# Layer two with tokens as the stationary operand, weights converted by their bits, exponentials slot by slot, and filler matmuls at the start

## The chip, the cores and the metric

The kernel runs on one core of a Trainium2 chip. The metric is the time of one execution in device microseconds, and the median of three runs is taken. A core has five engines that run their own instruction streams in order and wait for each other on semaphores: PE (TensorE, matmuls; its weight loads are shown as PEld), DVE (VectorE), ACT (ScalarE), POOL (GpSimd) and SP (SyncE, which here only issues DMAs).

## What is computed

Eight batches of 576 tokens pass through windowed attention with 8 heads of 64 and then through a gated two-layer network. Heads 0 to 3 look at the last 32 keys; heads 4 to 7 look at every fourth of the last 128 keys (dilated).

```python
scores = scale * np.matmul(q, k.transpose(0, 1, 3, 2))
scores = np.where(masks[None, :, :, :], scores, -1000000000.0)
scores = scores - np.max(scores, axis=-1, keepdims=True)
attn = np.exp(scores)
attn = attn / (np.sum(attn, axis=-1, keepdims=True) + 1e-09)
x = np.matmul(attn, v)                 # heads side by side: [8, 576, 512]
h = np.maximum(x @ w_in, 0.0)          # [8, 576, 1024]
conv_out = sum(conv_w[k] * hp[:, k:k + S, :] for k in range(3))   # hp: h padded by a zero row
gate = 1.0 / (1.0 + np.exp(-conv_out))
return h * gate @ w_out                # [8, 576, 512]
```

The three weight tensors come as 64-bit floats and are passed to the chip as pairs of 32-bit words.

## The kernel before

**Attention.** It works on pairs of heads, four pairs per batch: pairs 0 and 1 are plain (kind 0), pairs 2 and 3 dilated (kind 1). A pair is one piece of short matmuls for the scores (L248) into the PSUM tile `att`, a softmax on DVE and ACT in nine slots of 64 keys (L254 to L273), one piece of short matmuls for the values (L283), again into `att`, and copies that split the result into a high and a low part, `x..a` and `x..b` (L320, L333 to L337). `att` is one buffer, so scores and values take turns. For the first two batches (HELPED) the high part is subtracted on PE by matmuls with `minus`, a negated identity (L327, L330), and ACT copies the rest.

**The network.** Each product of two numbers is made of three terms (TERMS): high by high, high by low, low by high. Layer one (L353) has the weights stationary and 288 tokens moving: 8 blocks of the hidden width x 2 halves of the tokens x 4 slices x 3 terms = 192 matmuls per batch. ACT applies the relu into `h`, DVE and ACT make the convolution, the sigmoid and the gate, and `g..a` and `g..b` are its high and low parts. Layer two (L395) again has the weights stationary and 288 tokens moving: 4 x 2 x 8 x 3 = 192 matmuls per batch, with the output transposed. Over eight batches each layer has 1536 matmuls of 288 columns.

**The weights.** 16 blocks of 128x512 and the small `conv` are converted on ACT and DVE (`weights`, L413). For the first ten blocks (SUMMED) the low part is finished on PE: a 128x512 matmul in f32 (L450) and two in fp32r (L451, L452).

**The order.** Every piece of work is a task with a cost and a due time. `Planner.order` (L113) lists the tasks engine by engine from estimated costs, buffers and due times, and the program is written in that order. The due times are DUE, PAIR, WI and WO (L196 to L204). Outside the plan stand the first instructions: the DMA of the mask on ACT's queue, an identity, and five DVE copies that spread the mask (L465 to L479).

Of the kernel before, what the change touches and what calls it, by code (L numbers as in the profile page):

```python
# [34 lines left out]
F32 = mybir.dt.float32  # L35
# [10 lines left out]
NP = 4  # L46
# [27 lines left out]
class Planner:  # L74
# [38 lines left out]
    def order(self):  # L113
# [40 lines left out]
        return [t for _, t in sorted(done, key=lambda x: x[0])]  # L154
# [3 lines left out]
def attn_moe(ctx: ExitStack, tc: tile.TileContext, qk_p, qk_d, v_p, v_d, w_in, w_out, conv, mask, out):  # L158
# [37 lines left out]
    DUE = {0: (-9.2, 2.8, 30.4), 1: (64.7, 50.1, 92.3)}  # L196
    PAIR = {0: (-26.0, -24.7, -23.0, -27.0), 1: (-4.9, 1.3, 8.9, 14.5)}
    WI, WO = (-20.4, -20.4, -7.2, -7.2, -3.1, -0.1, 7.8, 7.8), (17.2, 17.2, 36.3, 36.3, 36.9, 34.9, 43.2, 43.2)
    AHEAD = (9.1, 0.8, 0.7)
    PERIOD = 55.1  # L200
    for b in range(2, B):
        DUE[b] = tuple(t + PERIOD * b for t in (-5.1, 5.4, 33.0))
        PAIR[b] = tuple(t + PERIOD * b for t in (-21.7, -18.8, -17.2, -13.1))
    SUMMED = 10  # L204
    HELPED = 2

# [21 lines left out]
    def attention(b, p):  # L228
        due = PAIR[b][p]
# [5 lines left out]
        lq = plan.add("SP", n * 0.0017, due - AHEAD[0], lambda: nc.sync.dma_start(  # L235
            out=qk.t[:, :n], in_=(qk_p, qk_d)[kind][b, p % 2]), uses=[qk])
        lv = plan.add("SP", 1.35, due - AHEAD[1], lambda: nc.sync.dma_start(
            out=v.t, in_=(v_p, v_d)[kind][b, p % 2]), uses=[v])

        def scores():  # L240
# [11 lines left out]
        flat = lambda: s.t.rearrange("p a k -> p (a k)")  # L252
        halves = lambda t: t.rearrange("p (h k) -> p h k", h=2)
        last = plan.add("DVE", 0.68, due + 1.5, lambda: nc.vector.tensor_tensor(  # L254
            out=halves(flat()[:, 0:512]), in0=sc.t[:, 0:2, 0:256], in1=halves(mask_sb[:, kind, 0:512]), op=ALU.add),
            [last], [sc, s])
        last = plan.add("DVE", 0.215, due + 1.5, lambda: nc.vector.tensor_tensor(  # L257
            out=flat()[:, 512:576], in0=sc.t[:, 2, 0:W], in1=mask_sb[:, kind, 512:576], op=ALU.add), [last], [sc, s])
        wide = lambda t: t.unsqueeze(2).to_broadcast([128, 9, W])
        last = plan.add("DVE", 0.755, due + 2.0, lambda: nc.vector.tensor_reduce(  # L260
            out=m.t, in_=s.t, axis=AX.X, op=ALU.max), [last], [s, m])
        last = plan.add("DVE", 0.755, due + 2.5, lambda: nc.vector.tensor_tensor(
            out=s.t, in0=s.t, in1=wide(m.t), op=ALU.subtract), [last], [s, m])
        last = plan.add("ACT", 0.685, due + 3.0, lambda: nc.scalar.activation(
            out=s.t, in_=s.t, func=AF.Exp, scale=SCALE), [last], [s], "exp")
        last = plan.add("DVE", 0.755, due + 3.5, lambda: nc.vector.tensor_reduce(
            out=z.t, in_=s.t, axis=AX.X, op=ALU.add), [last], [s, z])
        last = plan.add("DVE", 0.173, due + 3.6, lambda: nc.vector.tensor_scalar(
            out=z.t, in0=z.t, scalar1=1e-9, scalar2=None, op0=ALU.add), [last], [z])
        last = plan.add("DVE", 0.215, due + 3.7, lambda: nc.vector.reciprocal(out=z.t, in_=z.t), [last], [z])  # L270
        last = plan.add("DVE", 0.755, due + 3.8, lambda: nc.vector.tensor_tensor(  # L271
            out=s.t, in0=s.t, in1=wide(z.t), op=ALU.mult), [last], [s, z])
        last = plan.add("DVE", 0.755, due + 4.5, lambda: nc.vector.transpose(out=pt.t, in_=flat()), [last], [s, pt])  # L273
# [29 lines left out]
        last = plan.add("PE", (0.9, 0.85)[kind], due + 6.0, values, [lv, last], [v, pt, tv, x], "V")  # L303

        def parts(t):

            if kind == 0:
                return (t[:, 0:512].rearrange("c (q m) -> c q m", q=4), t[:, 512:S].rearrange("c (g m) -> c g m", g=2))
            t = t.rearrange("c (m r) -> c r m", r=RES)
            return t[:, :, 0:128], t[:, :, 128:RL].rearrange("c (g r) m -> c g r m", g=2)  # L310

        def src(i):
            if i == 0:
                return tv.t[:, :, 0:128]
            rest = tv.t[:, 0:2, 128:160]
            return rest if kind == 0 else rest.rearrange("c g (r m) -> c g r m", r=2)

        his = []
        for i, cost in ((1, (0.25, 0.3)[kind]), (0, (0.62, 1.12)[kind])):
            last = plan.add("ACT", cost, due + 7.0, lambda i=i: nc.scalar.copy(out=parts(x.t[0])[i], in_=src(i)),  # L320
                            [last, *his], [tv, x])
            his.append(last)
        if b < HELPED:
            def less():
                main, rest = parts(x.t[0])
                for t in range(4):
                    nc.tensor.matmul(tv.t[:, t, 0:128], minus, main[:, t], start=False, stop=True,  # L327
                                     skip_group_check=True)
# [3 lines left out]
            last = plan.add("PE", (0.42, 0.6)[kind], due + 7.2, less, his, [tv, x], "E")
            return [plan.add("ACT", cost, due + 7.5, lambda i=i: nc.scalar.copy(out=parts(x.t[1])[i], in_=src(i)),  # L333
                             [last], [tv, x]) for i, cost in ((0, (0.62, 1.12)[kind]), (1, (0.25, 0.3)[kind]))]
        return [plan.add("DVE", cost, due + 7.5, lambda i=i: nc.vector.tensor_tensor(
            out=parts(x.t[1])[i], in0=src(i), in1=parts(x.t[0].bitcast(F32))[i], op=ALU.subtract), his, [tv, x])
            for i, cost in ((0, (0.68, 1.0)[kind]), (1, (0.215, 0.25)[kind]))]  # L337
# [3 lines left out]

    def expert(b, ready, wired, wored, conved):
        due, gated, out_due = DUE[b]
        x = [xs[b, p] for p in range(NP)]
        h, c, g = ([Buffer(n) for _ in range(NF)] for n in "hcg")
        relu = []
        for u in range(2 * NF):
# [3 lines left out]
            def first(fc, hf, ps, k):  # L351
                for i, (jw, jx) in enumerate(TERMS):
                    nc.tensor.matmul(ps.t[:, 0:HALF], wi[jw][fc][:, k * 128:k * 128 + 128],  # L353
                                     x[k].t[jx][:, hf * HALF:hf * HALF + HALF],
                                     start=(k == 0 and i == 0), stop=(k == NC - 1 and i == 2))

            for k in range(NC):
                last = plan.add("PE", 0.396, due + 1.6 * u + 0.4 * k, lambda a=(fc, hf, ps, k): first(*a),
                                [last, wired[fc], *(ready[k] if b == 0 else sum(ready, []))], [ps, x[k]], "E")
# [9 lines left out]
        for fc in range(NF):  # L369
# [4 lines left out]
            for k in (0, 2):  # L374
# [5 lines left out]
            hi = plan.add("ACT", 0.675, d + 2.0, lambda fc=fc: nc.scalar.copy(out=g[fc].t[0], in_=c[fc].t),  # L380
                          [t], [c[fc], g[fc]])
            lo = plan.add("DVE", 0.755, d + 2.5, lambda fc=fc: nc.vector.tensor_tensor(
                out=g[fc].t[1], in0=c[fc].t, in1=g[fc].t[0].bitcast(F32), op=ALU.subtract), [hi], [c[fc], g[fc]])
            gates.append(lo)

        for dm in range(NC):
            o = Buffer("out")
            outs = []
            for hf in range(2):
                u = 2 * dm + hf  # L390
                ps, last = Buffer("nn"), None

                def second(dm, hf, ps, k):
                    for i, (jw, jg) in enumerate(TERMS):
                        nc.tensor.matmul(ps.t[:, 0:HALF], wo[jw][2 * dm + k // 4][:, k % 4 * 128:k % 4 * 128 + 128],  # L395
                                         g[k].t[jg][:, hf * HALF:hf * HALF + HALF],
                                         start=(k == 0 and i == 0), stop=(k == NF - 1 and i == 2))

                for k in range(NF):
                    last = plan.add("PE", 0.396, out_due + 3.3 * u + 0.4 * k, lambda a=(dm, hf, ps, k): second(*a),  # L400
                                    [last, wored[2 * dm + k // 4], gates[k]], [ps, g[k]], "E")
# [11 lines left out]
    def weights(src, n, due, dst=None, pair=None, summed=False):  # L413
# [10 lines left out]
        def step(cost, uses, run):  # L424
            return plan.add("DVE", 0.16 + cost * f, due, run, [last], uses)
# [141 lines left out]
```

## Time and profile before

| what | value |
|---|---|
| time, median of 3 runs (lowest, highest) | 549.82 us (549.78, 550.69) |
| span of the profiled execution, first to last instruction | 549.1 us |
| its busy time: PE, DVE, ACT | 522.4, 415.7, 298.1 us |
| DMA | 52.31 MB, mean 95 GB/s |

The time of the profiled execution itself is not listed apart from its span; the span is 0.7 us below the median of the runs. Times in rows of the timeline count from the start of the span. A matmul's record runs from its start to its modelled end, and consecutive ones overlap, so its price in a stream is the distance from start to start. One f32 matmul is two records, so "x72" is 36 matmuls; some records are missing.

### The profile page before, as it was taken

To read this page: it belongs to the slowest core of one execution; us is meant where nothing else is said; L and a number is where in the kernel's file an instruction comes from. 1 tells how busy PE (TensorE), PEld (TensorE's weight loads), DVE (VectorE), ACT (ScalarE), POOL (GpSimd) and SP (SyncE) were. 2 spreads that over 40 slices of the span, in tenths; PEclk is the share of its full clock that TensorE was granted. 3 is DMA by queue.
4 is the path that set the end of the run, shared out by engine and by line. 5 is a ranking of instruction groups with operands and counts; after the bars stand their busy time and mean duration, and the time that the engine had idled before them with its cause. 6 is when DMAs were issued, how large, how long until landed. Compare 5 with 4: busy or idle time off the path is not lost.

```text
span 549.1 us, 19084 instructions
## 1 busy us (share of the span) xinstructions
PE 522.4 (95%) x8664; PEld 497.2 (91%) x8664; DVE 415.7 (76%) x695; ACT 298.1 (54%) x556; POOL 0.9 (0%) x12
## 2 busy tenths in 40 slices
PE   3499978999999999999999999999999999999997
PEld 2468876999999999999999999999989999999997
DVE  4968998899997389946998389946988389946920
ACT  2457784855752486337742486237742486337721
POOL 0000000000000000000000000000000000000000
PEclk9999996999999999999999999999999999999999
DMA  7756513331044102630055102530045102300011
GB/s 247 268 157 215 195 52 137 119 121 44 7 138 152 30 23 65 200 110 23 13 161 170 32 23 72 190 113 23 17 152 162 45 23 58 117 26 23 0 44 44
DMA packets 17072, 52.31 MB, mean 95 GB/s; under 512 B 2016, under 2 KB 3168, under 8 KB 16992
## 3 DMA queue, kind: packets, MB, share of 16 engines
q1 hardware_dynamic: 16848, 51.02, 27.8%
q8 instruction: 68, 1.11, 0.9%
q10 hardware_dynamic: 144, 0.08, 0.1%
q14 instruction: 12, 0.10, 0.1%
HBM read 41.66 MB, written 9.44 MB: 93 GB/s over the span
## 4 chain that ended last, share of the span: by engine, by line
PE 92%; DVE 3%; ACT 2%; DMA 2%; issue 1%; ACTq 0%
PE nn L395 38%; PE mm L353 35%; PE att L283 8%; PE att L248 6%; PE nn L450 2%; PE nn L353 2%; PE att L327 1%; DMA qk<-in_qk_d_dram 1%; DMA qk<-in_qk_p_dram 1%; PE nn L451 0%; PE nn L452 0%; DVE pt L273 0%; DVE s L271 0%; PE att L330 0%; DVE c L365 0%
## 5 line engine op out<-in xcount | busy, mean ns | idle before, releaser
L365 DVE SCALAR_TENSOR_TENSOR c<-h,conv_sb,c 128x576 f32<-128x576 f32 x128 | 103.9, 815 | 48.4 <-ACT c L371 46.9
L360 ACT ACTIVATE h<-mm 128x288 f32<-128x288 f32 x120 | 48.8, 408 | 50.4 <-PE mm L353 50.1
L402 ACT COPY out<-nn 128x288 f32<-128x288 f32 x64 | 25.5, 400 | 70.1 <-PE nn L395 66.1
L378 DVE TENSOR_TENSOR c<-c,h 128x576 f32<-128x576 f32 x64 | 47.6, 755 | 9.4 <-ACT c L376 7.8
L283 PEld LDWEIGHTS att<-pt,v 32*64 32x64 f32 x3072 | 40.8, 138 | 14.8 <-DVE s L257 4.6
L283 PE MATMUL att<-pt,v 32*64 32x64 f32 (+2 forms) x3072 | 44.2, 232 | 9.4 <-DVE s L257 3.5
L371 ACT ACTIVATE c<-h,conv_sb 128x576 f32<-128x576 f32 x64 | 49.7, 776 | 1.3
L248 PE MATMUL att<-qk 64*32 64x64 f32 x2432 | 36.2, 235 | 11.0 <-DMA qk<-in_qk_d_dram 5.5
L248 PEld LDWEIGHTS att<-qk 64*32 64x32 f32 x2432 | 30.2, 111 | 16.9 <-DMA qk<-in_qk_d_dram 5.5
L376 ACT ACTIVATE c<-c 128x576 f32<-128x576 f32 x64 | 42.5, 678 | 2.1 <-DVE c L365 1.6
L353 PE MATMUL mm<-x2a,wi 128*128 128x288 f32 x144 | 40.5, 296 | 0.0
L353 PE MATMUL mm<-x1a,wi 128*128 128x288 f32 x144 | 40.3, 296 | 0.0
L353 PE MATMUL mm<-x3a,wi 128*128 128x288 f32 x144 | 40.3, 295 | 0.0
L353 PE MATMUL mm<-x0a,wi 128*128 128x288 f32 x144 | 40.3, 295 | 0.0
L395 PE MATMUL nn<-g2a,wo 128*128 128x288 f32 x128 | 37.0, 304 | 0.0
L395 PE MATMUL nn<-g0a,wo 128*128 128x288 f32 x128 | 36.4, 299 | 0.2
L395 PE MATMUL nn<-g6a,wo 128*128 128x288 f32 x128 | 36.6, 299 | 0.0
L395 PE MATMUL nn<-g3a,wo 128*128 128x288 f32 x128 | 36.4, 299 | 0.0
L395 PE MATMUL nn<-g1a,wo 128*128 128x288 f32 x128 | 36.4, 299 | 0.0
L395 PE MATMUL nn<-g4a,wo 128*128 128x288 f32 x128 | 36.4, 299 | 0.0
L395 PE MATMUL nn<-g5a,wo 128*128 128x288 f32 x128 | 36.4, 299 | 0.0
L395 PE MATMUL nn<-g7a,wo 128*128 128x288 f32 x128 | 36.1, 300 | 0.1
(194 smaller groups left out, 1502.5 us busy)
## 6 DMA issues: line engine op xcount, KB each, us to landing
qk<-in_qk_d_dram SPq DMA_DIRECT2D x16, 664.0 KB, 4.4
qk<-in_qk_p_dram SPq DMA_DIRECT2D x16, 592.0 KB, 4.9
out_dram<-out SPq DMA_DIRECT2D x28, 288.0 KB, 2.2
v<-in_v_d_dram SPq DMA_DIRECT2D x16, 384.0 KB, 3.4
v<-in_v_p_dram SPq DMA_DIRECT2D x16, 384.0 KB, 3.5
out<-in_w_in_dram SPq DMA_DIRECT2D x8, 512.0 KB, 4.5
out<-in_w_out_dram SPq DMA_DIRECT2D x8, 512.0 KB, 4.2
out_dram<-out SPq DMA_DIRECT2D x8, 144.0 KB, 1.8
```

The costliest lines, as they stand in the source:

```text
L248: nc.tensor.matmul(sc.t[quad * 32:quad * 32 + 32, slot // 4, slot % 4 * W:slot % 4 * W + W], q, k, start=i == 0, stop=i == len(parts) - 1, ...
L283: nc.tensor.matmul(tv.t[hd * 64:hd * 64 + 64, bank, o:o + n], v.t[quad * 32:quad * 32 + 32, block // 2, block % 2 * 64:block % 2 * 64 + 64 ...
L327: nc.tensor.matmul(tv.t[:, t, 0:128], minus, main[:, t], start=False, stop=True, skip_group_check=True)
L353: nc.tensor.matmul(ps.t[:, 0:HALF], wi[jw][fc][:, k * 128:k * 128 + 128], x[k].t[jx][:, hf * HALF:hf * HALF + HALF], start=(k == 0 and i = ...
L360: relu.append(plan.add("ACT", 0.4, due + 1.6 * u + 1.6, lambda fc=fc, hf=hf, ps=ps: nc.scalar.activation(out=h[fc].t[:, 1 + hf * HALF:1 + ...
L365: nc.vector.scalar_tensor_tensor(out=c[fc].t, in0=h[fc].t[:, k:S + k], scalar=conv_sb[:, k, fc:fc + 1], in1=c[fc].t, op0=ALU.mult, op1=ALU ...
L371: t = plan.add("ACT", 0.777, d, lambda fc=fc: nc.scalar.activation(out=c[fc].t, in_=h[fc].t[:, 1:S + 1], func=AF.Copy, scale=conv_sb[:, 1, ...
L376: t = plan.add("ACT", 0.686, d + 1.0, lambda fc=fc: nc.scalar.activation(out=c[fc].t, in_=c[fc].t, func=AF.Sigmoid), [t], [c[fc]], "sigmoid")
L378: t = plan.add("DVE", 0.755, d + 1.5, lambda fc=fc: nc.vector.tensor_tensor(out=c[fc].t, in0=c[fc].t, in1=h[fc].t[:, 1:S + 1], op=ALU.mult ...
L395: nc.tensor.matmul(ps.t[:, 0:HALF], wo[jw][2 * dm + k // 4][:, k % 4 * 128:k % 4 * 128 + 128], g[k].t[jg][:, hf * HALF:hf * HALF + HALF], ...
L402: outs.append(plan.add("ACT", 0.4, out_due + 3.3 + 3.3 * u, lambda hf=hf, ps=ps, o=o: nc.scalar.copy(out=o.t[:, hf * HALF:hf * HALF + HALF ...
L450: nc.tensor.matmul(ps.t, ident, t(), start=True, stop=False)
```

## The change

1. **Layer two** (L431 to L464 of the new kernel): 128 tokens of `g` are stationary and 512 columns of `w_out` move. The first batch does it in two halves of 256 columns. Two consecutive batches share the tiles `g`: the even one leaves its first 64 tokens there, and the odd one joins them with its own first 64 into one block of 128 tokens. Together there are 768 matmuls of 512 columns and 192 of 256. The output is written as tokens by width.
2. **Weights** (`weights`, L491): 8 blocks of 128x1024, and the three PE matmuls are gone. High and low parts are cut out by shifts, masks and one multiplication. `conv` has its own steps (`few_weights`).
3. **Softmax** of the first eight pairs, two batches (SLOTS): the maximum goes into the exponential as a per-partition bias, slot by slot, in nine ACTIVATE of 64 columns that also sum. The subtraction and the sum on DVE are gone for these pairs. For the other 24 pairs 1e-9 stands in a 65th column, and the sum takes it in.
4. **Copies** of the dilated pairs into `x` and out of it are walked in another order of axes.
5. **Fillers** (`filled`, `fill`): where the plan has PE idle in its first 90 us, bf16 matmuls of 256 columns with an identity `eye` go into an unread part of `att`. There are 192 of them, 173 ahead of the first matmul of layer one.
6. **Due times**: a table DUE with one number for each task.

```diff
+    def filled(self, done, fill, since, until, unit, slack):
+        at, more = since, []
+        for s, t in done:
+            if t.engine == "PE" and s < until:
+                n = int((s - at - slack) / unit)
+                if n > 0:
+                    more.append((at, Task("PE", n * unit, at, lambda n=n: fill(n), (), (), None)))
+                at = s + t.cost
...
+        if slotwise:
+            last = plan.add("ACT", 0.23, soft + 1.0, lambda: nc.scalar.mul(out=m.t, in_=m.t, mul=SCALE), [last], [m])
+
+            def exps():
+                for i in range(9):
+                    nc.scalar.activation(out=s.t[:, i, 0:W], in_=s.t[:, i, 0:W], func=AF.Exp, bias=m.t[:, i:i + 1],
+                                         scale=SCALE, accum_out=z.t[:, i:i + 1])
...
-                        nc.tensor.matmul(ps.t[:, 0:HALF], wo[jw][2 * dm + k // 4][:, k % 4 * 128:k % 4 * 128 + 128],
-                                         g[k].t[jg][:, hf * HALF:hf * HALF + HALF],
...
+                    nc.tensor.matmul(ps.t[:, 0:n], g[k // 2].t[:, k % 2, jg, c0:c0 + 128],
+                                     w.rearrange("p h c -> p (h c)") if hf is None else w[:, hf],
...
-            def add():
-                nc.tensor.matmul(ps.t, ident, t(), start=True, stop=False)
-                nc.tensor.matmul(ps.t, minus, r.t, start=False, stop=False)
-                nc.tensor.matmul(ps.t, minus, hi, start=False, stop=True)
...
+        left = step(0.69, [load], lambda: nc.vector.tensor_scalar(
+            out=bits(lw), in0=bits(lw), scalar1=9, scalar2=None, op0=ALU.logical_shift_right))
+        left = step(1.22, [left], lambda: nc.vector.scalar_tensor_tensor(
+            out=bits(lw), in0=bits(hw), scalar=23, in1=bits(lw), op0=ALU.logical_shift_left, op1=ALU.bitwise_or))
+        last = step(0.69, [top, left], lambda: nc.vector.tensor_scalar(
+            out=bits(hw), in0=bits(t), scalar1=-0x800000, scalar2=None, op0=ALU.bitwise_and))
...
+    nc.vector.tensor_copy(out=eye, in_=ident)
...
+            nc.tensor.matmul(att[:, 3, 256:512], eye, eye.unsqueeze(1).to_broadcast([128, 2, 128]), start=not begun,
+                             stop=True, skip_group_check=True)
...
-        for t in plan.order():
+        for t in plan.filled(plan.order(), fill, 2.0, 90.0, 0.109, 0.35):
```

The first place is PE's start. Before, its stream begins with the four scores pieces of the first batch and the first values piece (`qk` queries and keys, `pt` transposed weights of the softmax, `v` values):

```order
L248 MATMUL att_159<-qk_98 32x64 x40
L248 MATMUL att_159<-qk_99 32x64 x36
L248 MATMUL att_159<-qk_98 32x64 x36
L248 MATMUL att_159<-qk_99 32x64 x40
L283 MATMUL att_159<-pt_112,v_100 64x64 x24
```

Now pairs of a weight load and a filler stand ahead of each piece; the lines left out are such pairs alone, 15 fillers ahead of the first scores, 13 and 34 ahead of the next two:

```order
L558 LDWEIGHTS eye
L558 MATMUL att_125<-eye 128x256
...
L270 MATMUL att_125<-qk_80 32x64 x36
L558 LDWEIGHTS eye
L558 MATMUL att_125<-eye 128x256
...
L270 MATMUL att_125<-qk_81 32x64 x40
L558 LDWEIGHTS eye
L558 MATMUL att_125<-eye 128x256
...
L270 MATMUL att_125<-qk_80 32x64 x40
```

So the first scores stand behind 15 matmuls that read `eye`.

The second place is DVE's start. Before, the five mask copies are followed at once by the first softmax:

```order
L476 COPY mask_sb<-kinds_sb 128x64
L254 TENSOR_TENSOR s_103<-att_159,mask_sb 128x512
L257 TENSOR_TENSOR s_103<-att_159,mask_sb 128x64
L260 TENSOR_REDUCE m_106<-s_103 128x9
L262 TENSOR_TENSOR s_103<-s_103,m_106 128x576
```

Now the six steps of `conv` (tiles `few`) and the copy that makes `eye` stand between:

```order
L540 COPY mask_sb<-c_117 128x64
L479 TENSOR_SCALAR few_78<-few_78 128x24
L480 TENSOR_SCALAR few_79<-few_78 128x24
L482 SCALAR_TENSOR_TENSOR few_79<-few_raw,few_79 128x24
L484 TENSOR_SCALAR few_78<-few_79 128x24
L486 SCALAR_TENSOR_TENSOR few_78<-few_raw,few_78 128x24
L488 TENSOR_TENSOR conv_sb<-few_79,few_78 128x24
L531 CAST eye<-pt_94 128x128
L282 TENSOR_TENSOR s_85<-att_125,mask_sb 128x8x64
L282 TENSOR_TENSOR s_85<-att_125,mask_sb 128x64
```

So `eye` comes after the mask copies and after `conv`, on the engine that everything at the start needs.

The third place is layer two on PE in the second half of the program. Before, three matmuls per slice of the hidden width, 288 columns each:

```order
L395 MATMUL nn_163<-g5a,wo_89 128x288
L395 MATMUL nn_163<-g5b,wo_89 128x288
L395 MATMUL nn_163<-g5a,wo_97 128x288
L395 MATMUL nn_163<-g6a,wo_89 128x288
L395 MATMUL nn_163<-g6b,wo_89 128x288
```

Now, with 512 columns (a row with x2 is the high and the low part of `g`, which are one tile):

```order
L443 MATMUL nn_129<-wo_74,g_112 128x512 x2
L443 MATMUL nn_129<-wo_76,g_112 128x512
L443 MATMUL nn_129<-wo_74,g_113 128x512 x2
L443 MATMUL nn_129<-wo_76,g_113 128x512
L443 MATMUL nn_128<-wo_73,g_110 128x512 x2
```

Where before four blocks of the output width had two halves of the tokens each, there are now four or five blocks of tokens, each as wide as the output.

More of the change, by code (lines that the diff above doesn't have):

```diff
@@ L273, in attention @@
-        last = plan.add("DVE", 0.755, due + 4.5, lambda: nc.vector.transpose(out=pt.t, in_=flat()), [last], [s, pt])
+        flat = lambda: s.t[:, :, 0:W]
+        halves = lambda t: t.rearrange("p (h a) k -> p h a k", h=2)
+        scored = lambda: (sc.t[:, 0:2, 0:256].rearrange("p h (a k) -> p h a k", k=W), sc.t[:, 2, 0:W])
+        two = lambda t: (halves(t[:, 0:8]), t[:, 8])
+        masked = mask_sb[:, kind].rearrange("p (a k) -> p a k", k=W)
+        wide = lambda t: t.unsqueeze(2).to_broadcast([128, 9, W])
@@ L275, in values @@
+        last = plan.add("DVE", 0.215, soft + 2.2, lambda: nc.vector.reciprocal(out=z.t, in_=z.t), [last], [z])
+        last = plan.add("DVE", 0.755, soft + 2.3, lambda: nc.vector.tensor_tensor(
+            out=flat(), in0=flat(), in1=wide(z.t), op=ALU.mult), [last], [s, z])
+        last = plan.add("DVE", 0.775, soft + 3.0, lambda: nc.vector.transpose(
+            out=pt.t.rearrange("p (a k) -> p a k", k=W), in_=flat()), [last], [s, pt])
         def values():
@@ L332, in attention @@
[L332 to L335, printed above, removed]
+                    nc.tensor.matmul(tv.t[:, g, 128:160], minus,
+                                     rest[:, g] if kind == 0 else rest[:, :, g].rearrange("c m r -> c r m"), start=False,
+                                     stop=True, skip_group_check=True)
@@ L336, in attention @@
+            last = plan.add("PE", 0.6, val + 1.2, less, his, [tv, x], "E")
+            return [plan.add("ACT", cost, val + 1.5, lambda i=i: nc.scalar.copy(out=parts(x.t[1])[i], in_=src(i)),
+                             [last], [tv, x]) for i, cost in pieces]
+        return [plan.add("DVE", cost + 0.06 * (1 - i), val + 1.5, lambda i=i: nc.vector.tensor_tensor(
             out=parts(x.t[1])[i], in0=src(i), in1=parts(x.t[0].bitcast(F32))[i], op=ALU.subtract), his, [tv, x])
-            for i, cost in ((0, (0.68, 1.0)[kind]), (1, (0.215, 0.25)[kind]))]
+            for i, cost in pieces]
@@ L384, in expert @@
             gates.append(lo)
[L386 to L395, printed above, removed]
-                                         g[k].t[jg][:, hf * HALF:hf * HALF + HALF],
[L397 to L401, printed above, removed]
-                outs.append(plan.add("ACT", 0.4, out_due + 3.3 + 3.3 * u, lambda hf=hf, ps=ps, o=o: nc.scalar.copy(
-                    out=o.t[:, hf * HALF:hf * HALF + HALF], in_=ps.t[:, 0:HALF]), [last], [ps, o]))
-                if b == B - 1:
-                    plan.add("SP", 0.6, out_due + 4.0 + 3.3 * u, lambda dm=dm, hf=hf, o=o: nc.sync.dma_start(
-                        out=out[b, dm, :, hf * HALF:hf * HALF + HALF], in_=o.t[:, hf * HALF:hf * HALF + HALF]),
-                        [outs[-1]], [o])
-            if b < B - 1:
-                plan.add("SP", 1.2, out_due + 4.0 + 6.6 * dm, lambda dm=dm, o=o: nc.sync.dma_start(
-                    out=out[b, dm], in_=o.t[:, :S]), outs, [o])
@@ new lines, in few_weights, with step @@
+    def few_weights(src, due):
+        u, t = few
+        low, high = (few_raw[:, :, i] for i in range(2))
+        ui, ti = u.bitcast(I32), t.bitcast(I32)
+        def step(run, after, engine="DVE"):
+            return plan.add(engine, 0.2, due, run, [after])
+        last = plan.add("SP", 0.1, due - 2.0, lambda: nc.sync.dma_start(
+            out=few_raw, in_=src.bitcast(I32).rearrange("p (n t) -> p n t", t=2)))
+        last = step(lambda: nc.scalar.activation(out=u, in_=high.bitcast(F32), func=AF.Abs), last, "ACT")
+        last = step(lambda: nc.vector.tensor_scalar(out=u, in0=u, scalar1=2.0 ** -15, scalar2=None, op0=ALU.max), last)
+        last = step(lambda: nc.vector.tensor_scalar(
+            out=ti, in0=ui, scalar1=3, scalar2=0x3fffffff, op0=ALU.logical_shift_left, op1=ALU.bitwise_and), last)
+        last = step(lambda: nc.vector.scalar_tensor_tensor(
+            out=ti, in0=high, scalar=-0x40000000, in1=ti, op0=ALU.bitwise_and, op1=ALU.bitwise_or), last)
+        last = step(lambda: nc.vector.tensor_scalar(
+            out=ui, in0=ti, scalar1=-0x800000, scalar2=None, op0=ALU.bitwise_and), last)
+        last = step(lambda: nc.vector.scalar_tensor_tensor(
+            out=u, in0=low.bitcast(U32), scalar=2.0 ** -52, in1=u, op0=ALU.mult, op1=ALU.mult), last)
+        return step(lambda: nc.vector.tensor_tensor(
+            out=conv_sb.rearrange("p t c -> p (t c)"), in0=t, in1=u, op=ALU.add), last)
@@ new lines, in weights, with step @@
+    def weights(src, due, fetch, hi, lo):
+        raw, tb = Buffer("raw"), Buffer("t")
+        part = lambda i: raw.t.rearrange("p (n w) -> p n w", w=2)[:, :, i]
+        lw, hw = (lambda i=i: part(i).bitcast(F32) for i in range(2))
+        t = lambda: tb.t
+        shaped = lambda x, like: x.rearrange("p (a c) -> p a c", a=like.shape[1])
+        whole = lambda x: x.rearrange("p a b c -> p a (b c)") if len(x.shape) == 4 else x
+        hi, lo = whole(hi), whole(lo)
+        bits = lambda x: x().bitcast(I32)
+        load = plan.add("SP", 3.0, fetch, lambda: nc.sync.dma_start(
+            out=raw.t, in_=src.bitcast(I32)), uses=[raw])
+        def step(cost, after, run):
+            return plan.add("DVE", cost, due, run, after, [raw, tb])
+        last = plan.add("ACT", 1.14, due, lambda: nc.scalar.activation(out=t(), in_=hw(), func=AF.Abs), [load], [raw, tb])
+        last = step(0.69, [last], lambda: nc.vector.tensor_scalar(
+            out=t(), in0=t(), scalar1=2.0 ** -15, scalar2=None, op0=ALU.max))
+        last = step(0.69, [last], lambda: nc.vector.tensor_scalar(
+            out=bits(t), in0=bits(t), scalar1=3, scalar2=0x3ffff000,
+            op0=ALU.logical_shift_left, op1=ALU.bitwise_and))
+        top = step(1.22, [last], lambda: nc.vector.scalar_tensor_tensor(
+            out=bits(t), in0=bits(hw), scalar=-0x40000000, in1=bits(t), op0=ALU.bitwise_and, op1=ALU.bitwise_or))
+        high = plan.add("ACT", 1.14, due, lambda: nc.scalar.copy(out=hi, in_=shaped(t(), hi)), [top], [tb])
+        left = step(0.69, [load], lambda: nc.vector.tensor_scalar(
[4 more added lines that the diff above has]
+            out=bits(hw), in0=bits(t), scalar1=-0x800000, scalar2=None, op0=ALU.bitwise_and))
+        return [high, plan.add("DVE", 1.22, due, lambda: nc.vector.scalar_tensor_tensor(
+            out=lo, in0=shaped(lw().bitcast(U32), lo), scalar=2.0 ** -43, in1=shaped(hw(), lo),
+            op0=ALU.mult, op1=ALU.mult), [last], [raw])]
@@ L465, in attn_moe @@
+    ident = pts[0][0][:, 0:128]
+    kinds_sb = cs[0][0].bitcast(BF16)[:, 0:5 * W].rearrange("p (a k) -> p a k", k=W)
     nc.scalar.dma_start(out=kinds_sb, in_=mask)
```

243 lines of the change are left out of this document (127 added, 116 removed).

## Prediction

> **What bounds the kernel now.** I read the page from the top: span, busy times, slices, the chain of work that ended last.
>
> ```profile
> span 549.1 us, 19084 instructions
> PE 522.4 (95%) x8664; PEld 497.2 (91%) x8664; DVE 415.7 (76%) x695; ACT 298.1 (54%) x556; POOL 0.9 (0%) x12
> PE   3499978999999999999999999999999999999997
> PE 92%; DVE 3%; ACT 2%; DMA 2%; issue 1%; ACTq 0%
> ```
>
> PE carries 92% of the chain and is short of 9 tenths only in the first slices and the last. A busy PE is not yet PE doing needed work, so the windows come next (length; busy time and instructions by engine; granted clock, DMA).
>
> ```profile
> 0.00:98.66 98.66, 76.82 (x1672) 64.91 (x1673) 82.72 (x161) 57.95 (x109) 0.90 (x12) 0.95 0.52 180
> 98.66:140.00 41.34, 41.34 (x377) 41.08 (x377) 38.03 (x65) 25.86 (x48) 0.00 (x0) 1.00 0.25 85
> 305.80:367.45 61.65, 61.65 (x1074) 59.68 (x1074) 47.25 (x76) 33.33 (x62) 0.00 (x0) 1.00 0.27 89
> ```
>
> From 98.66 us PE never rests; a steady batch takes 61.65 us, with DVE at 47.25 and ACT at 33.33. So there are two stages: a start that DVE, ACT and DMAs shape, and a body that only PE's own work shortens. I therefore count that work at its steady price and call the rest lost. From the chain in order of time (start, length, what, matmuls):
>
> ```profile
> 38.80 1.29 PE att L283 x81
> 114.61 19.09 PE nn L395 x144
> 333.63 0.90 PE att L248 x58
> 342.39 1.06 PE att L248 x66
> 347.22 1.19 PE att L283 x77
> ```
>
> One matmul of 288 columns costs 19.09 / 144 = 0.1326 us; both layers have 2 x 1536, so 407.3 us. Scores cost 0.90 (plain) or 1.06 (dilated), values 1.29 or 1.19; two of each in eight batches make 16 x 4.44 = 71.0 us. Returning from such a piece costs more, as PE's timeline shows:
>
> ```profile
> 333.33 0.29 PE L395 MATMUL nn<-g1a,wo 128*128 128x288 f32 x1
> 333.56 0.97 PE L248 MATMUL att<-qk 64*32 64x64 f32 x72
> 334.46 0.40 PE L395 MATMUL nn<-g2a,wo 128*128 128x288 f32 x1
> 334.70 0.29 PE L395 MATMUL nn<-g2b,wo 128*128 128x288 f32 x1
> ```
>
> 333.33 to 334.70 is 1.37 us; less 0.90 and two starts of 0.13 that leaves 0.2 us. Both orders have 55 returns: 11.0 us. The weight sums and the subtractions by `minus`:
>
> ```profile
> 28.04 2.08 PE L450 MATMUL nn<-w0b,ident 128*128 128x512 f32 x2
> 30.76 1.89 PE L450 MATMUL nn<-w1b,ident 128*128 128x512 f32 x2
> 48.82 1.02 PE L450 MATMUL nn<-w0b,ident 128*128 128x512 f32 x2
> 49.91 0.39 PE L452 MATMUL nn<-wi,minus 128*128 128x512 f32 x1
> 50.14 0.29 PE L353 MATMUL mm<-x1a,wi 128*128 128x288 f32 x1
> 97.90 0.63 PE L327 MATMUL att<-x1a,minus 128*128 128x128 f32 x4
> 98.51 0.38 PE L395 MATMUL nn<-g0a,wo 128*128 128x288 f32 x1
> ```
>
> One weight sum takes 48.82 to 50.14, 1.32 us, ten of them 13.2. A subtraction takes 97.90 to 98.51, 0.61 us, eight of them 4.9. **PE's work before** is 407.3 + 71.0 + 11.0 + 13.2 + 4.9 = 507.4 us. The last matmul ends at 545.6 (tail, below), so **38.2 us are lost**, nearly all before 98.66 us. Part of that is a slow clock: the same three matmuls of a sum took 28.04 to 30.76, 2.72 us, 2.06 times the later price.
>
> **The change, part by part.** The **weight sums** go: -13.2 us of PE.
>
> **Layer two** becomes 768 matmuls of 512 columns and 192 of 256. The trace has a 512-column fp32r matmul: 49.91 to 50.14, 0.23 us. Against 0.1326 at 288 that is 0.000435 us per column, so 256 columns cost 0.1187. 768 x 0.23 + 192 x 0.1187 = 199.4, against 1536 x 0.1326 = 203.7: -4.3 us. Starts are printed to 0.01, so 0.225 to 0.235 bounds it: -8.1 to -0.5. I take the row.
>
> PE's work after is 507.4 - 13.2 - 4.3 = 489.9 us. In the body I expect no new waits: a layer-two block now lasts 24 x 0.23 = 5.5 us instead of 3.2, so two open blocks cover the last gate's chain better, and ACT's wider copies have its slack to hide in.
>
> **The start** is the uncertain part. First, `eye`. Rows of DVE, PE and ACT, then groups (count, busy, mean ns):
>
> ```profile
> 5.47 1.61 PE L248 MATMUL att<-qk 64*32 64x64 f32 x80 [5.47 <-DMA qk<-in_qk_d_dram]
> 5.64 0.45 DVE L472 COPY mask_sb<-kinds_sb 128x576 bf16<-128x576 bf16 x1 [5.64 <-DMA kinds_sb<-in_mask_dram]
> 6.60 0.17 DVE L476 COPY mask_sb<-kinds_sb 128x64 bf16<-128x64 bf16 x1
> 39.32 0.23 ACT L428 ACTIVATE w0a<-out 128x24 f32<-128x24 f32 x1
> 39.58 0.18 DVE L430 TENSOR_SCALAR w0a<-w0a 128x24 f32<-128x24 f32 x1 [1.00 <-ACT w0a L428]
> 40.73 0.18 DVE L457 TENSOR_TENSOR conv_sb<-w0b,w0a 128x24 f32<-128x24 f32 x1
> ```
>
> ```profile
> L371 ACT ACTIVATE c<-h,conv_sb 128x576 f32<-128x576 f32 x64 | 49.7, 776 | 1.3
> L376 ACT ACTIVATE c<-c 128x576 f32<-128x576 f32 x64 | 42.5, 678 | 2.1 <-DVE c L365 1.6
> L264 ACT ACTIVATE s<-s 128x576 f32<-128x576 f32 x32 | 21.3, 684 | 21.8 <-DVE s L262 21.7
> L262 DVE TENSOR_TENSOR s<-s,m 128x576 f32<-128x576 f32 x32 | 24.1, 753 | 0.7
> L433 DVE TENSOR_SCALAR w0b<-w0a 128x512 int32<-128x512 int32 x8 | 3.4, 423 | 0.3
> L435 DVE SCALAR_TENSOR_TENSOR w1b<-out,w1b 128x512 int32<-128x512 int32 x8 | 5.5, 686 | 0.1
> ```
>
> The mask lands at 5.64 and its copies end at 6.77. The six steps of `conv` then take 39.58 to 40.91, 1.3 us, and the cast of `eye` about 0.2, so `eye` exists near 8.3 us. Only then can the 15 fillers run that stand ahead of the first scores, though the queries could be there at 5.47. Cold, at 2.06 x 0.1187 = 0.245 each, they last 3.7 us. **The first scores start near 12 us instead of 5.47**, and the DMAs that wait to reuse `qk` shift with them.
>
> How soon the fillers warm PE up: before, PE worked nearly without a gap from 26 us and ran a 512-column matmul in 0.39 at 32.7 us, some 6.5 us later. The Trainium skill, "TensorE: Matmul & The Clock Gate", Part 1, has PE at half clock until about 3.4 us of sustained work; by it the first 15 fillers would nearly do, by the trace some 12 more run cold, 1.5 us. Both lie inside my range.
>
> Second, **all 192 fillers** take 192 x 0.1187 = 22.8 us of PE, whatever they cover. With `eye` the floor of the loss is 8.3 + 22.8 = 31 us (29 if a bf16 filler has no fixed part and costs 256 / 288 of 0.1187).
>
> Third, the chains. Slot-wise, a pair loses DVE's subtraction (0.753) and a sum of like width. It gains nine 64-column exponentials for one of 684 ns. From 24 to 576 columns ACT goes from 230 to 684 ns, so 64 columns cost 263, and a per-partition operand adds 776 - 678 = 98. Starts of neighbours overlap by some 90, so 0.27 each, up to 0.47 if the sum adds a read; I take 0.3, the nearer end: 2.7 us a pair, 2 us longer on ACT. A weight block has four TENSOR_SCALAR and three two-source steps of 1024 columns. At twice the slope of the rows that is 0.68 and 1.22 us, 6.4 us of DVE, 51 us for eight blocks, about what 16 small ones cost before; but two of the four walk every second word, which no row shows. If that halves their rate they cost 1.2, +8.5 us over all; at the rows' price nothing. I take the rows.
>
> Walking the new orders with these prices, each row starting when its engine and operands are free, the fourth values piece ends near 46 us (before: 38.80 + 1.29 = 40.1). PE's work by then is five scores, four values and three subtractions, 11.7 us, so 34 us are lost. The 19 later fillers (2.3 us) and some 3 us of waits for ACT, which interleaves exponentials, copies and relus, make 39. Before lost more after that point: 2.97 us idle at once, and a cold clock behind it:
>
> ```profile
> 81.98 0.25 PE L283 MATMUL att<-pt,v 32*64 32x32 f32 x3 [2.97 <-DVE pt L273]
> 545.66 0.40 ACT L402 COPY out<-nn 128x288 f32<-128x288 f32 x1 [2.80 <-PE nn L395]
> 546.09 0.33 SPq L405 DMA_DIRECT2D out_dram<-out x1
> ```
>
> Between the floor, 31, and the walk, 39, I take **37 us lost**, nearer the walk. The **tail**, 545.6 to 549.1, is 3.5 us; copy and store of 512 columns instead of 288 add at most 0.5: 4.0.
>
> **Sum:** 489.9 + 37 + 4.0 = 530.9 us of span, 18.2 less than 549.1. With the 0.7 us between span and median: **531.6 us**.
>
> **Rivals.**
> - *The start costs no more than its floor* (DVE steps overlap better than I walked): loss 29 to 31, 523.6 to 525.6 us; with the cheapest 512 columns 520. For it: the fillers were counted from planned gaps. Against: planned gaps end before the real DMAs do.
> - *Dearer steps at the start*: strided steps at 1.2 us and exponentials at 0.47 (72 x 0.17 = 12 us of ACT), half of it on the path: loss 45 to 52, 540 to 547 us.
> - *Layer two is no cheaper*: 512 columns cost 512 / 288 of 0.1326, 0.2357. Then the 4.3 us stay: 536 us. Against it stands the 0.23 row.
> - *Slower*: the fillers do not warm PE up and each delays what is queued behind it. 192 x 0.245 = 47 us and 8.3 for `eye` make 55; with 5 us of waits, loss 60 and 554.6 us. It decides from a loss of 55.2 us on. For it: the clock was slow at 28 us despite work since 20. Against: it was fast from 33 us on.
> - *The matmul's price does not follow its columns.* Then 512 cost 0.1326 too: 74.8 us less, 457 us. The 0.23 row speaks against it, and layer one does not tell. In a sentence by itself: the Trainium skill, same page, Back-to-back issue gap, gives about 131 ns for 512 columns in a stream with weight loads, which the 0.23 us here contradicts.
>
> **How the numbers follow.** Forecast, 525.6 to 538 us: 0.57; layer two no cheaper: 0.05; floor: 0.14; dearer start: 0.18; slower: 0.04; within 0.2%, about what a measurement of this kernel can tell from no change: 0.01; price without columns: 0.01. The range 521 to 542 holds the forecast, layer two no cheaper, nearly all of the floor and a third of the dearer start, about 0.8. Faster 0.95, same 0.01, slower 0.04.
>
> **What will show it.** Right: no f32 matmul of 512 columns; layer-two starts 0.23 us apart; a steady batch near 61.1 us (61.65 - 4.3 / 8); first scores at 11 to 13 us behind fillers; the fourth values near 46 us. Wrong: first scores near 5 us; starts other than 0.225 to 0.235 apart; idle PE beyond 130 us; strided steps near 1.2 us; fillers 0.24 us apart after 20 us.

## The result, and the profile after

The changed kernel takes 552.57 us (median of 6 runs, 551.97 to 554.61) against 549.80 us for the one before: ratio 1.0052, with a 95% interval of 1.0036 to 1.0069. It is slower by half a per cent, where 531.6 us were forecast. Some executions show a lower granted clock and a time more than 1.5% above the fastest; they are left out of all medians and ratios here (three of apart_waits, one of halves_all). From the page of the changed kernel: span, busy times, PE's 40 slices, the chain that ended last by engine.

```profile
span 551.2 us, 18203 instructions
PE 522.3 (95%) x8240; PEld 460.6 (84%) x8240; DVE 397.9 (72%) x612; ACT 304.3 (55%) x660; POOL 1.0 (0%) x15
PE   4767999999999999998999999999999999999997
PE 88%; DVE 4%; DMA 3%; ACT 3%; issue 2%; SPq 0%; ACTq 0%
```

PE is as busy as before (522.3 against 522.4 us), though it has less to do; the fillers make up the difference. The chain in order of time (start, length, what, how many) tells where the time went:

```profile
7.78 3.38 PE att L558 x15
11.16 1.27 PE att L270 x70
12.43 1.78 PE att L558 x13
14.23 0.83 DVE s L282 x2
15.11 1.13 PE att L270 x65
16.24 3.83 PE att L558 x34
20.10 0.83 DVE s L282 x2
...
35.06 1.36 PE att L318 x81
36.42 1.10 PE att L558 x9
37.55 0.71 ACT x0a L356 x2
38.30 0.72 PE att L363 x4
39.15 0.81 PE att L558 x7
...
46.61 1.66 PE att L318 x78
...
55.00 1.25 PE att L318 x69
...
519.92 27.32 PE nn L443 x117
547.30 0.59 ACT out L453
```

Read it downward. Scores (L270) end at 12.43. DVE's add, which reads them and needs nothing else, starts at 14.23, when 13 fillers have ended; the next add waits for 34 fillers, until 20.10. With the values (L318) it is the same: ACT's copy starts after the fillers, at 37.55, not at 36.42. **The fillers are links of the chain.** They were to lie beside the step on DVE or ACT, and they lie ahead of it. DVE's own rows name what it waited for:

```profile
14.23 0.82 DVE L282 TENSOR_TENSOR s<-att,mask_sb 128x512 f32<-128x512 f32 x2 [6.51 <-PE att L558]
20.10 0.82 DVE L282 TENSOR_TENSOR s<-att,mask_sb 128x512 f32<-128x512 f32 x2 [4.25 <-PE att L558]
```

The fillers write columns 256 to 511 of the fourth bank of `att`; the add reads the first three banks. No number passes between them, but both name the same tile, and the add's semaphore wait covers the last write to it that stands ahead in the program, a filler.

The fourth values piece ends at 56.25 (before: 40.09). Layer two begins at 111.00, and from 111.17 to the end of the last matmul PE is busy for 433.33 of 436.07 us.

### The profile page after: what moved, and what is told of

It is laid out like the page before. It is cut to its first block, busy times and chain, and to the rows that moved or that the text cites. A ratio compares the mean times of both kernels' runs of the same rounds, so it can differ in the third digit from the quotient of the medians.

```text
span 551.2 us, 18203 instructions
## 1 busy us (share of the span) xinstructions
PE 522.3 (95%) x8240; PEld 460.6 (84%) x8240; DVE 397.9 (72%) x612; ACT 304.3 (55%) x660; POOL 1.0 (0%) x15
## 4 chain that ended last, share of the span: by engine, by line
PE 88%; DVE 4%; DMA 3%; ACT 3%; issue 2%; SPq 0%; ACTq 0%
PE nn L443 37%; PE mm L398 31%; PE att L318 7%; PE att L270 5%; PE att L558 4%; PE nn L398 2%; DMA qk<-in_qk_d_dram 1%; DMA c<-in_mask_dram 1%; DMA v<-in_v_d_dram 1%; PE att L363 1%; DVE s L282 1%; DVE c L410 1%; DMA v<-in_v_p_dram 1%; ACT c L421 1%; ACT h L405 0%
## 5 line engine op out<-in xcount | busy, mean ns | idle before, releaser
L443 PE MATMUL nn<-wo,g 128*128 128x512 f32 (+1 forms) x960 | 212.0, 375 | 0.0
L443 PEld LDWEIGHTS nn<-wo,g 128*128 128x128 f32 x960 | 163.3, 188 | 33.5 <-DVE wo L522 0.2
L453 ACT COPY out<-nn 128x512 f32<-128x512 f32 (+1 forms) x40 | 21.7, 542 | 71.8 <-PE nn L443 44.8
L425 ACT CAST g<-c 128x576 fp32r<-128x576 f32 x64 | 42.5, 672 | 17.7 <-DVE c L423 15.7
L318 PEld LDWEIGHTS att<-pt,v 32*64 32x64 f32 x3072 | 39.0, 132 | 14.2 <-issue 9.5
L427 DVE TENSOR_TENSOR g<-c,g 128x576 fp32r<-128x576 f32 x64 | 47.6, 755 | 3.9 <-ACT g L425 2.8
L282 DVE TENSOR_TENSOR s<-att,mask_sb 128x512 f32<-128x512 f32 x64 | 26.7, 451 | 27.7 <-PE att L270 13.9
L318 PE MATMUL att<-pt,v 32*64 32x64 f32 (+2 forms) x3072 | 42.3, 226 | 4.4 <-DVE s L282 0.9
L270 PEld LDWEIGHTS att<-qk 64*32 64x32 f32 x2432 | 28.8, 106 | 16.2 <-issue 7.1
L270 PE MATMUL att<-qk 64*32 64x64 f32 x2432 | 34.2, 226 | 7.4 <-DVE s L282 4.5
L398 PE MATMUL mm<-x6a,wi 128*128 128x288 f32 x128 | 36.6, 301 | 0.2
L398 PE MATMUL mm<-x5a,wi 128*128 128x288 f32 x128 | 36.2, 298 | 0.2 <-ACT h L405 0.2
L398 PE MATMUL mm<-x4a,wi 128*128 128x288 f32 x128 | 35.9, 295 | 0.0
L558 PE MATMUL att<-eye 128*128 128x256 bf16 x192 | 26.6, 294 | 9.4 <-DVE eye L531 7.8
## 6 DMA issues: line engine op xcount, KB each, us to landing
out_dram<-out SPq DMA_DIRECT2D x28, 256.0 KB, 2.4
```

Of the source, the lines that this page charges most:

```text
L270: nc.tensor.matmul(sc.t[quad * 32:quad * 32 + 32, slot // 4, slot % 4 * W:slot % 4 * W + W], q, k, start=i == 0, stop=i == len(parts) - 1, ...
L318: nc.tensor.matmul(tv.t[hd * 64:hd * 64 + 64, bank, o:o + n], v.t[quad * 32:quad * 32 + 32, block // 2, block % 2 * 64:block % 2 * 64 + 64 ...
L398: nc.tensor.matmul(ps.t[:, 0:HALF], wi[jw][fc // 2][:, fc % 2, k], x[k].t[jx][:, hf * HALF:hf * HALF + HALF], start=(k == 0 and i == 0), s ...
L443: nc.tensor.matmul(ps.t[:, 0:n], g[k // 2].t[:, k % 2, jg, c0:c0 + 128], w.rearrange("p h c -> p (h c)") if hf is None else w[:, hf], star ...
L558: nc.tensor.matmul(att[:, 3, 256:512], eye, eye.unsqueeze(1).to_broadcast([128, 2, 128]), start=not begun, stop=True, skip_group_check=True)
```

## The experiments

"A" is the theory that the fillers stand in the chain, "B" that they lie where PE would wait anyway, and that dearer steps on ACT and DVE took the time. The kernels below the first two rows are edits of the changed kernel. Times are medians in us; "values" is the end of the fourth values piece, "layer two" its first matmul, "end" the end of the last matmul, each in the profiled execution. The profiled execution of halves_all took 554.94 us and that of apart_early_half 537.62, so these two rows lie late against their medians.

| kernel | time | ratio to before (95%) | first scores | values | layer two | end |
|---|---|---|---|---|---|---|
| before | 549.8 | | 5.47 | 40.09 | 94.44 | 545.58 |
| changed | 552.57 | 1.0036 to 1.0069 | 11.09 | 56.25 | 111.00 | 547.22 |
| no_fill | 535.84 | 0.9734 to 0.9759 | 4.96 | 40.59 | 95.02 | 529.99 |
| fill_apart | 541.92 | 0.9846 to 0.9875 | 10.90 | 45.14 | 101.08 | 535.75 |
| apart_waits | 551.74 | 1.0013 to 1.0061 | 11.03 | 54.31 | 109.56 | 545.97 |
| eye_early | 544.15 | 0.9890 to 0.9919 | 5.07 | 47.55 | 102.31 | 538.14 |
| apart_early | 536.99 | 0.9755 to 0.9808 | 5.11 | 38.29 | 94.42 | 529.88 |
| apart_early_half | 535.31 | 0.9714 to 0.9762 | 4.99 | 42.95 | 96.37 | 531.75 |
| apart_early_capped | 535.99 | 0.9721 to 0.9770 | 5.16 | 38.05 | 92.94 | 528.13 |
| no_fill_one_exp | 534.59 | 0.9705 to 0.9738 | 4.90 | 40.33 | 94.00 | 529.39 |
| halves_all | 548.60 | 0.9976 to 1.0037 | 10.72 | 59.75 | 116.65 | 549.15 |
| no_fill_halves | 536.58 | 0.9736 to 0.9782 | 4.87 | 40.14 | 95.39 | 531.04 |

### no_fill: without the fillers

```diff
-        for t in plan.filled(plan.order(), fill, 2.0, 90.0, 0.109, 0.35):
+        for _, t in plan.order():
```

> All 192 short bf16 matmuls are left out; they feed nothing, so the output is the same work. Theory A, each run of them stands in the chain (the add on DVE or the copy on ACT that reads scores or values starts only when the run behind them has ended): about 24 us of runs and 2.3 us of waiting for eye go, and a slow clock gives 6 to 10 us back on scores, values and subtractions before the first layer one: 532 to 540 us. Theory B, the runs lie where PE would wait anyway, and the time went into dearer steps of ACT and DVE: the runs turn into idle PE, 549 to 556 us.

535.84 us, as A says: the fillers cost 16.7 us net. What they do buy is seen too. PE's rows of no_fill:

```profile
22.67 2.06 PE L318 MATMUL att<-pt,v 32*64 32x64 f32 x96 [0.95 <-DVE s L282]
25.52 1.12 PE L363 MATMUL att<-x0a,minus 128*128 128x128 f32 x4 [0.79 <-ACT x0a L356]
27.77 2.06 PE L318 MATMUL att<-pt,v 32*64 32x64 f32 x96 [0.79 <-ACT x0b L371]
```

A values piece takes 2.06 us there and 1.36 with fillers, four `minus` matmuls 1.12 instead of 0.72: without the fillers PE stays slow until after the fourth values. The granted clock of the profile does not show it, it reads 1.00 from 0 to 40.59 us; the durations do. The slowness just costs less than the fillers.

### fill_apart and apart_waits: the same fillers in another tile

```diff
+            into = spare[:, 0:256] if len(begun) < 173 else att[:, 3, 256:512]
-            nc.tensor.matmul(att[:, 3, 256:512], eye, ...
+            nc.tensor.matmul(into, eye, ...
```

`spare` is the second `mm` buffer, which nothing reads until layer one.

> The first 173 short matmuls write a PSUM tile that nothing reads yet (the second mm) instead of att. They stay where they are on PE. Theory A: the add or copy behind each run starts at the end of the scores, values or subtractions instead of the end of the run, so some 15 runs lie beside a step of 0.7 to 0.9 us that now follows them: 537 to 543 us, and DVE's first add starts near 12.5 us instead of 14.23. Theory B: 551 to 554 us.

541.92 us, 10.7 us less, with the same instructions in the same order. DVE's first adds in fill_apart:

```profile
12.04 0.82 DVE L282 TENSOR_TENSOR s<-att,mask_sb 128x512 f32<-128x512 f32 x2 [4.51 <-PE att L270]
12.90 0.76 DVE L284 TENSOR_REDUCE m<-s 128x9 f32<-128x576 f32 x1
14.63 0.82 DVE L282 TENSOR_TENSOR s<-att,mask_sb 128x512 f32<-128x512 f32 x2 [0.97 <-PE att L270]
```

They wait for the scores (L270) and no longer for L558; the second comes 5.5 us earlier (14.63 against 20.10). But fill_apart also takes the fillers' writes out of the banks that DVE and ACT read. To tell the wait from the bank, the last filler of each run goes back to `att`:

```diff
-            into = spare[:, 0:256] if len(begun) < 173 else att[:, 3, 256:512]
+            into = spare[:, 0:256] if len(begun) < 173 and i < n - 1 else att[:, 3, 256:512]
```

> As fill_apart, but the last matmul of each run of the first 173 writes att as before, so the add or copy that reads scores or values waits for the run's end again, while all others still write the idle mm tile. If that wait is what fill_apart removed, the time is back near the changed kernel's 552.6: 551 to 554 us. If fill_apart gained because the short matmuls left the PSUM banks that DVE and ACT read, it stays near 541.9: 541 to 544 us.

551.74 us: 9.8 of the 10.7 us are back, with 12 of the first 173 fillers in `att`; the interval (1.0013 to 1.0061) overlaps that of the changed kernel. In apart_waits DVE waits for the run's end again:

```profile
13.78 0.82 DVE L282 TENSOR_TENSOR s<-att,mask_sb 128x512 f32<-128x512 f32 x2 [6.12 <-PE att L559]
19.65 0.82 DVE L282 TENSOR_TENSOR s<-att,mask_sb 128x512 f32<-128x512 f32 x2 [4.25 <-PE att L559]
```

It is the wait, not the bank.

### eye_early: eye made on POOL

```diff
+    nc.gpsimd.tensor_copy(out=eye, in_=ident)
-    nc.vector.tensor_copy(out=eye, in_=ident)
```

> eye is made on POOL right behind the identity, near 2 us, instead of on DVE at 7.50. Both theories: first scores near 5.5 us instead of 11.1. If the start is one chain from there (A), DVE's first add is bound by the mask and conv steps, which end near 7.6, and by 13 matmuls: about 5 us less, 546 to 549 us. If another chain (loads of the weights, ACT) sets the end of the start, 551 to 553 us.

544.15 us, 8.4 us less, more than either outcome. From eye_early's chain:

```profile
7.60 0.83 DVE s L282 x2
39.42 1.26 PE att L318 x77
46.29 1.26 PE att L318 x76
```

DVE's first add starts at 7.60, where it was expected, but that is 6.6 us earlier than in the changed kernel (14.23), not 5. At the third values eye_early is 7.2 us ahead (39.42 against 46.61), at the fourth 8.7 (46.29 against 55.00). In between the changed kernel's profiled run has a stretch at half clock that eye_early's has not. Windows of the changed kernel (busy time of PE, PEld, DVE, ACT, POOL; then the granted clock):

```profile
47.00:50.40 3.40, 3.40 (x90) 2.71 (x75) 1.43 (x2) 2.54 (x16) 0.00 (x0) 0.51 0.30 94
```

PE was busy all the while; 3.4 us at half speed are some 1.7 us of work. The stretch explains little of the median, though: the run of the changed kernel with a mean granted clock of 1.0 took 552.12 us, still 8.0 above eye_early.

### apart_early, apart_early_half, apart_early_capped: do fillers pay at all?

The first has both edits. The second cuts every run of fillers to half, the third to at most 8:

```diff
-        for _ in range(n):
+        for _ in range((n + 1) // 2):        # half
+        for _ in range(min(n, 8)):           # capped
```

> Both edits at once: the first 173 short matmuls write the idle mm tile, and eye is made on POOL. Alone they gave 10.7 and 8.4 us. If the two costs are separate, 552.6 - 19.1 = 533.5 us, and the short matmuls then pay for themselves (without them 535.8). If both gains are partly the same chain, or eye_early also gained by the half-speed stretch of the clock that it missed (3.4 us, some 2 us of work), 535 to 538 us, and they do not pay.

> As apart_early, with every run of short matmuls cut to half, rounded up: 101 instead of 192. If half is enough to keep the clock up, the scores queued behind the runs start earlier, 531 to 534 us, and values pieces still take 1.3 us. If the clock falls, values pieces take 1.9 to 2.1 us and the time is near that without any, 535 to 537 us.

> As apart_early, with no run longer than 8 short matmuls (0.87 us, about the step that follows each piece): 93 before layer one. If the runs of 13 to 34 still delayed the scores, 533 to 535 us. If DVE's conversions of the weights set the end of the start, as apart_early's chain from 29 to 42 us says, no less than its 537.0 and no_fill's 535.8 within the noise: 535 to 538 us.

536.99, 535.31 and 535.99 us: their intervals overlap each other's and no_fill's. In apart_early_half the clock fell: the granted clock was 0.53 from 20 to 30 us and 0.50 from 30 to 40, and a values piece shows it:

```profile
30.13 2.05 PE L318 MATMUL att<-pt,v 32*64 32x64 f32 x96
```

In these three, fillers that delay nobody cost nothing that can be measured, and gain nothing. In apart_early the fourth values end 2.3 us before no_fill's, and layer two begins only 0.6 us earlier (94.42 and 95.02). Between lies work of DVE. The chain of apart_early:

```profile
29.18 0.78 DVE pt L307
29.96 0.64 DVE m L284
30.59 0.60 DVE raw L516
31.20 0.60 DVE t L508
31.80 1.13 DVE raw L518
...
37.38 1.11 DVE wi L522
...
42.62 0.82 DVE s L282 x2
```

and its window over that stretch:

```profile
29.18:42.62 13.44, 13.44 (x354) 11.87 (x354) 13.20 (x18) 9.29 (x34) 0.00 (x0) 1.00 0.64 219
```

DVE is busy 13.20 of 13.44 us, with softmax and the conversion of the weights in turn. The granted clock is 1.00 there and PE busy, part of it with fillers, while the chain runs on DVE. In this stretch a faster PE has nothing to give.

### no_fill_one_exp: are the slot-wise exponentials dear?

```diff
-                for i in range(9):
-                    nc.scalar.activation(out=s.t[:, i, 0:W], ..., bias=m.t[:, i:i + 1], scale=SCALE, accum_out=...)
+                nc.scalar.activation(out=flat(), in_=flat(), func=AF.Exp, scale=SCALE)
```

> No short matmuls, and in the slot-wise pairs one exponential of 576 columns stands for the nine of 64 columns; the row maximum is not subtracted and the sums are not taken, so the output is another. A pair costs ACT 0.68 instead of 3.1 us. If ACT's nine exponentials carry the start, as 9.2 us of them in the chain of no_fill say, 529 to 532 us; if DVE's steps are next in line at once, 534 to 536 us.

534.59 us, 1.3 us less than no_fill, the second of the two outcomes. The nine exponentials are dearer than thought, but next to nothing of that reaches the end. That 9.2 us of them stood in no_fill's chain misled: when they are shortened, another chain of about the same length remains. So of the two dearer steps that B could name, the exponentials are worth 1.3 us at most without the fillers, and the conversion steps on DVE cost what was forecast (below).

### halves_all and no_fill_halves: 256 columns instead of 512

```diff
-                    nc.tensor.matmul(ps.t[:, 0:n], g[k // 2].t[...], w.rearrange("p h c -> p (h c)") if hf is None else w[:, hf], ...)
+                    for part in range(n // 256):
+                        nc.tensor.matmul(ps.t[:, part * 256:part * 256 + 256], g[k // 2].t[...], w[:, part if hf is None else hf], ...)
```

> Each layer-two matmul of 512 columns is two of 256 with the same stationary tokens; the plan's order is the same. The first batch's 256-column starts lie 0.113 to 0.116 us apart, the others' 512-column starts 0.233. If price per column holds, 768 x (0.233 - 2 x 0.1133) = 5 us less: 547 to 548 us. If the weight load of each start bounds a stream of short matmuls, 552 us or more.

> No short matmuls, and each layer-two matmul of 512 columns as two of 256 with the same tokens; only the first of a block opens the accumulation in its bank. By 256-column starts of 0.1133 us against 0.233 for 512: 768 x 0.0064 = 5 us less than no_fill's 535.8: 530 to 532 us. If the records' 0.1133 does not hold in a long stream, 535 to 537 us.

In halves_all each half opens the accumulation in the bank, in no_fill_halves only the first does. The output of halves_all is off by 0.24 in relative terms; an estimate of what it would be off by if every first half lost its first product, one of eight slices in half of the columns, is the root of 1/16, 0.25. So the second opening seems to undo that product; the number of matmuls is the same.

halves_all takes 548.60 us, 4.0 less than the changed kernel and near the 5 expected, but its runs lie between 547.41 and 555.62 and the two intervals just touch; its profiled run had a granted clock of 0.53 from 40 to 50 us. no_fill_halves takes 536.58 us beside no_fill's 535.84: no gain, the second of its outcomes, and not for the reason given there. The last stretch of layer two, first in no_fill, then in no_fill_halves:

```profile
502.68 27.32 PE nn L443 x117
```

```profile
504.51 26.55 PE nn L444 x234
```

27.32 / 117 = 0.2335 us for 512 columns; two of 256 take 26.55 / 117 = 0.2269. So the price of 256 columns holds in a long stream, and by it 768 x 0.0066 = 5 us were to be had. The stretch begins 1.8 us later all the same, so the body gave them back before it. PE's listed waits from 95 us on are 3.8 us in no_fill_halves and 1.1 in no_fill, the longest of them 1.7 us ahead of layer one; the rest is not accounted for, and whether 256 columns pay stays open.

## Why the prediction was wrong, step by step

**Right.** The first scores: forecast near 12 us, measured 11.09; `eye` near 8.3, measured 7.7. A cold filler 0.245, measured 3.38 / 15 = 0.225; a warm one 0.1187, measured 3.83 / 34 = 0.113. DVE's strided steps cost the row's price, 0.68 forecast, and not 1.2. From the changed kernel's groups (the first writes every second word, the second reads and writes every second word):

```profile
L520 DVE TENSOR_SCALAR raw<-t 128x1024 int32<-128x1024 int32 x8 | 5.5, 693 | 0.2
L516 DVE TENSOR_SCALAR raw<-raw 128x1024 int32<-128x1024 int32 x8 | 5.5, 686 | 0.0
```

The sums on PE that go, layer two and the tail together make up no_fill's span, 15.1 us shorter than before's (534.0 against 549.1): 13.2 and 2.0 less, 0.5 more in the tail, and 0.4 left over.

**The step that failed** is this one: "Walking the new orders with these prices, each row starting when its engine and operands are free, the fourth values piece ends near 46 us". It ended at 56.25. The walk took the add and the copies as free to start when the scores or values were there. They also waited for the fillers behind, because these write the same tile. fill_apart, which has the fillers and not the wait, ends its fourth values at 45.14:

```profile
43.83 1.31 PE L318 MATMUL att<-pt,v 32*64 32x32 f32 x96
```

So the walk came out near 46 for the program that it walked, partly by luck: in that run the granted clock was 0.61 from 28 to 30 us and 0.54 from 30 to 32, and the exponentials were dearer than walked. Both lines that show the wait, the fillers' target `att` and the add's operand `att`, were in the diff and in the order; I read the first as a place that nobody reads, and asked only what the fillers cost PE. That wait is worth 10.7 of the 21.0 us between forecast and time; fill_apart without it still takes 541.92.

**Terms mis-sized.** Layer two: 768 x 0.2335, from the last stretch, and for 256 columns this stretch of the changed kernel's chain

```profile
122.39 11.16 PE nn L443 x96
```

192 x 0.1163: together 201.7, so 2.0 us saved instead of 4.3; the single distance of 0.23 from the trace was too short a ruler. PE's work is then 492.2 and 547.2 - 492.2 = 55.0 us are lost, 37 were forecast. By 56.25 PE had done 11.6 us (five scores, four values, three subtractions), so 44.6 of them lie there; the forecast had 34. The other 10.4 come later, where the forecast's 37 left 3. They are the second thing that the prediction had wrong ("In the body I expect no new waits"). Among them are the later fillers, waits of the later subtractions, and waits in the body such as this one of PE's waits after, at 254.4 to 256.0 us, where the prediction had named idle PE as a sign of being wrong:

```profile
PE att L270 <- DMA qk<-in_qk_d_dram: 1.7, 1, 1.7
```

By the same working fill_apart loses 10.0 us behind its fourth values (535.75 - 492.2 - 45.14 + 11.6) and no_fill, without any filler, 8.8 (529.99 - 492.2 - 40.59 + 11.6), so most of this loss does not come from fillers in `att`; what makes it up was not followed further. The kernel before had such losses behind its start as well, 2.97 us idle and then a granted clock of 0.50 from 84.0 to 93.5 us: I called its 38.2 us "nearly all before 98.66 us" and let the forecast's 37 stand for the start alone. So the 20.3 us between forecast and span are 10.6 in the start, 7.4 behind it and 2.3 in layer two's price.

**Slot-wise exponentials**: 0.3 us each forecast. Two groups of the changed kernel:

```profile
L291 ACT ACTIVATE s<-s,m 128x64 f32<-128x64 f32 x72 | 24.0, 336 | 0.2
L291 ACT ACTIVATION_READ_ACCUMULATOR s<-s,m 128x1 f32 x72 | 13.5, 187 | 0.0
```

Each sum brings an instruction of its own that reads the accumulator; the nine take 3.1 us a pair (16.12 to 19.22 us for the first), not 2.7.

**The rivals.** The slower one came nearest: 554.6 us, deciding from a loss of 55.2. That its 55 us for fillers and `eye` equal the 55.0 lost is luck: the fillers were busy for 26.6 us and not 47, and the rest was lost elsewhere. Half of its mechanism held, that each filler delays what is queued behind it; what was delayed was not only PE's own queue but DVE and ACT. Its other half, fillers that don't warm PE, did not occur. In the changed kernel the first scores, 3.3 us after the first filler, still take 1.27 us for x70, the 13 fillers behind them go at 1.78 / 13 = 0.137 each, and a run of 34 fillers soon after at 0.113; so full speed came roughly 5 us after the first filler. In eye_early the first scores, 3.1 us after it, are fast already:

```profile
5.07 0.97 PE L270 MATMUL att<-qk 64*32 64x64 f32 x72
```

By the Trainium skill ("TensorE: Matmul & The Clock Gate", Part 1) full clock comes after about 3.4 us of work, in windows that run freely and so start before or behind it. The traces agree that the point moves: roughly 5 us in the changed kernel, within 3.1 in eye_early, 6.5 read off the trace of before. The windows themselves no run here shows. The dearer start at 540 to 547 us had the place and the wrong cause. "Layer two is no cheaper" was about half right: 2.0 of the 4.3 us were saved. The floor was not reached: even no_fill lost 529.99 - 492.2 = 37.8 us. Two slips in the working had no weight: at 0.235 us layer two saves 0.4 us and not 0.5, and the rival without a price per column left out the 192 matmuls of 256 columns, 2.7 us more at 0.1326 than at 0.1187.

## What to carry to other kernels

In this program an instruction that writes a tile takes part in that tile's waits, whatever columns it touches; 12 fillers are enough for 9.8 us. So before costing a filler at "idle time of its engine", list who reads the tile and is queued behind it, and put it into a tile that nobody reads. Filling an engine's gaps can pay only if the chain runs through that engine; here DVE was next, and the four variants with harmless fillers or none end within 1.7 us of each other. These four are 2.2 to 2.6% faster than before (intervals from 1.9 to 2.9%): the change without its fillers, or with them in a tile of their own and `eye` made early.

## What the runs showed of the hardware

The clock can fall while PE works: 0.51 granted from 47.0 to 50.4 us, behind some microseconds in which PE ran values, subtractions and fillers with waits of 0.79 us for ACT between them, and not in eye_early, which runs the same pieces with waits of the same length. Why is open. In fill_apart it fell at 28 us (0.61 from 28 to 30), behind 2.27 us in which PE did nothing. A layer-two matmul of 512 columns costs slightly more (0.2335) than two of 256 (0.2269), with a weight load for each.
